# Loading q, k and v of the second group ahead of the weights, and issuing later q and k loads behind the transposing DMAs

## The chip, the cores and the metric

One core of a Trainium2 chip. The metric is the device time of one execution in microseconds (us); a time is the median of repeated runs, and the kernel before is timed on the same chip beside each variant.

The engines are called as in the profile: PE does matmuls, DVE vector work, ACT functions such as GELU (the profile of before has 21 table loads of 1.28 us, which come where the program changes the function), GpSimd (POOL) and SyncE (SP) issue DMAs here.

## The reference, cut to what matters

A gated linear attention runs over 4 batches of 768 positions, 8 heads of 48. Its output x (3072 tokens of 384) goes through a gated GELU layer of width 1536.

```python
for t in range(S):                                  # S = 768; the kernel takes 3 "groups" of 256 positions per batch, 12 in all
    S_re, S_im = a_t * (S_re, S_im) + k_t v_t^T     # complex decay a, after normalising |a|
    y_t = q_t . S_re
x   = y as 3072 x 384
out = x + sigmoid(x @ w_res) * ((gelu(x @ w_gate) * (x @ w_val)) @ w_out)
```

## The kernel before

q, k, a_re and a_im arrive as float32 rows of 48 numbers, so in pieces of 192 bytes. Group g needs a(g), q(g), k(g) and v(g). The a, q and k loads and the stores of `ot` are issued from SyncE's queue; v, the weights and the second stores to the output (`x`, added to what `ot` left) from GpSimd's. `held(..., after)` makes an issue wait until an earlier load has landed; `issue_after` only orders the building of the program.

```python
def ramp():                      # groups 0 to 4: decay, cumulative sums, first attention
    ...                          # -- cut --
    load_q(1, T["ld", "w", 1])   # q, k of group 1: behind the second pair of weight loads
    a0 = attention_first(g0, 0, 0)
    ...                          # -- cut: csl(g1), ex(g1), csl(g2), ex(g2), squares of groups 3, 4 --
    with tc.issue_after(T["row"].ins):
        load_q(2, T["ld", "w", 2])   # q, k of group 2: behind the third pair
    load_w_out()                     # w_out: behind q of group 2
    ...
    with tc.issue_after(T["ld", "k", 2].ins):
        load_a(5)

def mk(nm, src):                 # later groups: padded products, transposed by DMA
    ...
    if g >= TURN:                # TURN = 5
        nc.sync.dma_start_transpose(out=tt, in_=pads[nm, g % 2])   # QT, KT

for g in range(3):
    load_a(g)
load_q(0)
for g in gs(2):                  # groups 3 and 4
    load_a(g)
load_v(0, T["ld", "ai", 2])
for i in range(4):
    load_w_in(i, T["ld", "k", 0])     # a pair (w_gate, w_val) per i, behind k of group 0
load_v(1, T["ld", "w", 0])
load_w_res()
load_v(2, T["ld", "w", 1])
ramp()
for u in range(NU + 1):
    if u > 0:
        phase_x(u)               # output matmuls of unit u-1, decay sums of unit u+1
    ...
    phase_y(u)                   # gate and value matmuls of unit u, attention of unit u+1
    for g in gs(u + 2 if u == 0 else u + 3) + (gs(3) if u == 0 else []):
        load_q(g)                # two phases ahead
        after_landing(T["k", g], call(load_v, g))
```

There are 3 buffers for q and k. Units 1 to 5 hold two groups each. padQ and padK are the padded products of a group, QT and KT what the transposing DMAs make of them. I call the phase y of unit 0 "Y0", and the two in which transposes met other loads "Y2" and "Y3".

Of the kernel before, what the change touches and what calls it, by code (L numbers as in the profile page):

```python
# [28 lines left out]
def kernel(  # L29
# [13 lines left out]
    nc = tc.nc  # L43
# [55 lines left out]
    pads = {}  # L99
# [28 lines left out]
    T = {}  # L128
# [12 lines left out]
    def rows(a, g, c):  # L141
        b, s = ORD[g]
        t0 = (s * C + c) * 128
        return a[b, :, t0:t0 + 128, :].rearrange("h t d -> t h d")
# [4 lines left out]
    def held(i, after):  # L149

        if after is not None:
            tc.add_manual_dep(i.ins, after.ins.name, behind, reason="load order")
        return i

    def load_a(g, after=None):
        for nm, src, pool in (("ar", a_re, ldr), ("ai", a_im, lda)):
            t = pool.tile([128, C, H, D], FP, tag=nm, name=nm)
            for c in range(C):
                T["ld", nm, g] = held(nc.sync.dma_start(out=t[:, c], in_=rows(src, g, c)), after)  # L159
            T[nm, g] = t  # L160
        T["a"] = g + 1

    def load_q(g, after=None):
        for nm, src in (("q", q), ("k", k)):
            t = ldq.tile([128, C, H, D], FP, tag=nm, name=nm)
            for c in range(C):
                T["ld", nm, g] = held(nc.sync.dma_start(out=t[:, c], in_=rows(src, g, c)), after)
            T[nm, g] = t

    def load_v(g, after=None):  # L170
        t = ldv.tile([128, C, H, D], BF, tag="v", name="v")
        for c in range(C):
            held(nc.gpsimd.dma_start(out=t[:, c], in_=rows(v, g, c)), after)  # L173
        T["v", g] = t

    def load_w_in(i, after=None):

        FQ = FF // 4
        for w, src in ((wg, moe_w_gate), (wv, moe_w_val)):
            T["ld", "w", i] = held(nc.gpsimd.dma_start(  # L180
                out=w[:, :, i * FQ:(i + 1) * FQ],
                in_=src[:, i * FQ:(i + 1) * FQ].rearrange("(i p) m -> p i m", p=128)), after)
# [17 lines left out]
    def flat(t):  # L200
        return t.rearrange("p c h d -> p (c h d)")
# [31 lines left out]
    def p1_steps(g):  # L233

        def s0():
            lm = T["lm", g]
            act(out=lm, in_=lm, func=AF.Ln)
            nc.vector.tensor_scalar(out=lm, in0=lm, scalar1=0.5, scalar2=LNMAX, op0=OP.mult, op1=OP.min)  # L238

        def s1():  # L240
            ar = flat(T["ar", g])
            T["s", g] = pE.tile([128, W], FP, tag="E" if g == 1 else "Ei", name="ra") if g in (1, 2) else ar
            act(out=T["s", g], in_=ar, func=AF.Ln)

        def s2():
            T["th", g] = flat(T["ai", g])
            act(out=T["s", g], in_=T["s", g], func=AF.Exp, scale=-1.0)
            nc.vector.tensor_tensor(out=T["th", g], in0=T["s", g], in1=T["th", g], op=OP.mult)
        return [s0, s1, s2]
# [5 lines left out]
    def cs_l(g, c):  # L255
        if c == 0:
            if g == 0:
                t = hb.tile([128, 4, DM], FP, tag="sg", name="E0")
                T["E", g] = t[:, 0:2].rearrange("p a m -> p (a m)")
                T["Ei", g] = t[:, 2:4].rearrange("p a m -> p (a m)")  # L260
            else:
                T["E", g] = pE.tile([128, W], FP, tag="E", name="E")
                T["Ei", g] = pE.tile([128, W], FP, tag="Ei", name="Ei")
        sl = slice(c * DM, (c + 1) * DM)
        cs = psM.tile([128, DM], FP, tag="mm", padded_shape=[128, 512], name="csl")
        nc.tensor.matmul(out=cs, lhsT=lmat[c], rhs=T["lm", g][:, sl], start=True, stop=True)  # L266

        def ex():
            act(out=T["E", g][:, sl], in_=cs, func=AF.Exp)
            act(out=T["Ei", g][:, sl], in_=cs, func=AF.Exp, scale=-1.0)  # L270
        return ex
# [63 lines left out]
    def decay2(g):  # L335
        if g in NEXT.values():
            nc.gpsimd.dma_start(out=T["md", g][1:2, :], in_=T["Ei", g][0:1, 0:DM])
            turn("m2", g, T["md", g], 2)
        if g in NEXT:
            md = dr.tile([2, DM], FP, tag="d2", name="d2")  # L340
            T["row"] = (nc.sync if ORD[g][1] == 0 else nc.gpsimd).dma_start(out=md[0:1, :], in_=T["E", g][127:128, DM:W])
            T["md", NEXT[g]] = md
# [14 lines left out]
    def products(g):  # L357
        def x0():
            qE = flat(T["q", g]).bitcast(BF)[:, 0:W]
            nc.vector.tensor_tensor(out=qE, in0=flat(T["q", g]), in1=T["E", g], op=OP.mult)  # L360
            T["qE", g] = qE

        def x1():
            kE = flat(T["k", g]).bitcast(BF)[:, 0:W]
            nc.vector.tensor_tensor(out=kE, in0=flat(T["k", g]), in1=T["Ei", g], op=OP.mult)
            T["kE", g] = kE

        def mk(nm, src):
            def x():
                t = pads[nm, g % 2][:, :, 0:DD].rearrange("p x (u d) -> p x u d", u=2)  # L370
                sb = T[src, g].rearrange("p (x u d) -> p x u d", u=1, d=D).to_broadcast([128, C * H, 2, D])
                nc.vector.tensor_tensor(out=t, in0=T["CS", g], in1=sb, op=OP.mult)
                T[nm, g] = t
                if g >= TURN:
                    tt = trp.tile([128, C * H, 128], BF, tag=nm + "T", name=nm + "T")
                    nc.sync.dma_start_transpose(out=tt, in_=pads[nm, g % 2])
                    T[nm + "T", g] = tt
            return x
        return [x0, mk("Q", "qE"), x1, mk("K", "kE")]
# [247 lines left out]
    def gs(u):  # L627
        return UNITS[u] if 0 <= u < NU else []
# [7 lines left out]
    def call(f, *a):  # L636
        return lambda: f(*a)
# [56 lines left out]
    def ramp():  # L694

        g0, g1, g2 = gs(0) + gs(1)
        pend = {}

        def csl(g):
            pend[g] = [cs_l(g, c) for c in range(C)]  # L700

        def ex(g):
            for f in pend[g]:
                f()
            decay2(g)

        def cst(g):
            for c in range(C):
                cs_t(g, c)
        g3, g4 = gs(2)  # L710
        p = {g: p1_steps(g) for g in range(5)}
        q = {g: squares(g) for g in range(5)}
        pr = products(g0)

        def run(*fs):
            for f in fs:
                f()
        table("natural_log_exp_and_others")()
        run(*q[g0], p[g0][0], p[g0][1])
        csl(g0)  # L720
        run(p[g1][1], p[g0][2], q[g1][1], p[g1][2])
        ex(g0)
        run(p[g2][1], q[g2][1], p[g2][2])
        table("trig_and_small")()
        pr[0]()
        pr[2]()
        for g in (g0, g1, g2):
            if g > g0:
                T["f", g] = flat(T["ar", g])
            p1_arctan(g)  # L730
            cst(g)
            if g == g0:
                run(q[g1][0], q[g1][2], q[g2][0], q[g2][2])
        p2_sin(g0)
        pr[1]()
        pr[3]()
        load_q(1, T["ld", "w", 1])
        a0 = attention_first(g0, 0, 0)
        table("natural_log_exp_and_others")()
        run(p[g1][0], p[g2][0])  # L740
        run(*a0[:2])
        csl(g1)
        csl(g2)
        run(*a0[2:4], *q[g3], p[g3][1], p[g3][2])
        ex(g1)
        run(*a0[4:7], *q[g4], p[g4][1])
        ex(g2)
        run(p[g4][2], p[g3][0], p[g4][0], call(decay0, g4), *a0[7:])
        with tc.issue_after(T["row"].ins):
            load_q(2, T["ld", "w", 2])  # L750
        load_w_out()
        table("trig_and_small")()
        p2_sin(g1)
        p2_sin(g2)
        with tc.issue_after(T["ld", "k", 2].ins):
            load_a(5)
        p1_arctan(g3)
        p1_arctan(g4)
# [21 lines left out]
    load_q(0)  # L780
    for g in gs(2):
        load_a(g)
    load_v(0, T["ld", "ai", 2])
    for i in range(4):
        load_w_in(i, T["ld", "k", 0])
    load_v(1, T["ld", "w", 0])
    load_w_res()
    load_v(2, T["ld", "w", 1])
    ramp()
    for u in range(NU + 1):  # L790
        if u > 0:
            phase_x(u)
        while T["a"] < min(NG, gs(u + 1)[-1] + 6 if gs(u + 1) else NG):
            load_a(T["a"])
        phase_y(u)
        for g in gs(u + 2 if u == 0 else u + 3) + (gs(3) if u == 0 else []):
            load_q(g)
            after_landing(T["k", g], call(load_v, g))


# [28 lines left out]
```

## Time and profile before

| | before |
|---|---|
| timed median | 318.36 us (3 runs) |
| span in the profile | 315.3 us |
| first gate matmul (timeline of PE) | 58.6 us |
| ACT idle for ar, DVE idle for ai, of group 4 | 9.2 us, 12.9 us |
| PE idle for KT in Y2 and Y3 | 3.8 us, 3.0 us |
| Y2, Y3 (GELU table load to next table load) | 26.0 us, 25.7 us |

Some rows of the page's part 2. Each digit is a fortieth of the span (7.9 us): busy tenths, or tenths of the full TensorE clock.

```profile
PE   0355436789698999799599999598999998999994
DVE  0789119899599997699477999477995866565452
PEclk9998766599989999999979999899999999999999
DMA  8999999999999996369997259984479505920541
GB/s 150 187 178 187 177 147 190 179 189 177 155 179 130 188 189 89 39 121 236 192 185 61 46 92 216 190 154 28 74 121 183 93 2 106 181 49 2 126 77 51
```

DMA is busy until about 118 us. DVE has a hole at slices 5 and 6 (31 to 47 us), and PE one at slice 20 and one at slice 26.

The waits of the whole run; columns are total us, times, longest.

```profile
ACT lm L212 <- DMA ar<-in_a_re_dram: 14.7, 3, 9.2
DVE sq L223 <- DMA ai<-in_a_im_dram: 14.1, 3, 12.9
PE at L437 <- DMA KT<-padK: 6.8, 2, 3.8
```

The first two are the hole in the ramp, the third the holes in Y2 and Y3. Here is SyncE's queue as Y2 begins (start us, length us):

```profile
142.51 0.99 SPq L167 DMA_DIRECT2D q<-in_q_dram  x2
143.93 2.51 SPq L167 DMA_DIRECT2D k<-in_k_dram  x2
146.49 1.04 SPq L617 DMA_DIRECT2D out_dram<-ot  x1
147.57 3.18 SPq L376 DMA_TRANSPOSE QT<-padQ  x1
150.81 3.47 SPq L376 DMA_TRANSPOSE KT<-padK  x1
154.38 3.60 SPq L376 DMA_TRANSPOSE QT<-padQ  x1
158.08 2.65 SPq L376 DMA_TRANSPOSE KT<-padK  x1
```

padQ was ready at 142.5 us, yet QT is issued 5 us later, behind a q load, a k load and a store. The next lines are the windows view: stretch and its length, busy us and number of instructions of PE, PEld (weight loads), DVE, ACT and POOL, and behind them the granted clock (PEclk), DMA share (time of the packets over that of 16 engines; it can pass 1) and GB/s. First Y2, Y3 and the phase after them (Y4), then two stretches of Y2 around PE's wait, and two of Y3.

```profile
143.10:169.10 26.00, 21.84 (x154) 11.71 (x155) 19.23 (x35) 14.04 (x25) 6.20 (x9) 0.93 1.23 187
187.90:213.60 25.70, 21.94 (x149) 11.34 (x151) 18.65 (x35) 12.40 (x21) 6.98 (x9) 0.93 1.18 184
233.60:254.60 21.00, 20.84 (x155) 11.27 (x157) 15.53 (x29) 11.64 (x21) 1.71 (x2) 1.00 0.70 126
...
154.00:158.00 4.00, 0.17 (x2) 0.05 (x2) 0.80 (x5) 1.35 (x3) 1.32 (x2) 1.00 1.57 228
158.00:162.00 4.00, 3.78 (x22) 2.25 (x24) 2.31 (x5) 0.60 (x1) 0.00 (x0) 0.57 1.41 127
...
199.00:203.00 4.00, 0.98 (x7) 0.41 (x6) 1.55 (x6) 1.48 (x3) 1.35 (x2) 0.94 1.46 207
203.00:207.00 4.00, 3.78 (x24) 2.17 (x26) 2.23 (x5) 0.60 (x1) 0.00 (x0) 0.64 1.30 222
```

### The profile page before, as it was taken

The numbers are of one execution on the slowest core, as the hardware profiler recorded it, in microseconds if no ns is written. First come the engines' busy times: TensorE is split into PE (matmuls) and PEld (weight loads), VectorE is DVE, ScalarE is ACT, GpSimd is POOL, SyncE is SP. The second block draws the span as 40 slices with busy tenths as digits, with TensorE's granted clock in tenths as the row PEclk, the third lists the DMA queues.
The fourth block names the chain that finished last, engine by engine and source line by source line (L and its number), as shares of the span: only waits on it lengthen the run. The fifth ranks groups of instructions, "written<-read, shape, count | busy, mean of one in ns | idle before, by whom it ended". The sixth has DMA issues, their size and how long they took to land.

```text
span 315.3 us, 5310 instructions
## 1 busy us (share of the span) xinstructions
PE 258.6 (82%) x1912; PEld 156.2 (50%) x1928; DVE 229.0 (73%) x412; ACT 200.3 (64%) x333; POOL 89.9 (29%) x133
## 2 busy tenths in 40 slices
PE   0355436789698999799599999598999998999994
PEld 0133214578354666464256654265654565445682
DVE  0789119899599997699477999477995866565452
ACT  3867075979989578976548974359664474456150
POOL 4075300310337322462503555103711122110220
PEclk9998766599989999999979999899999999999999
DMA  8999999999999996369997259984479505920541
GB/s 150 187 178 187 177 147 190 179 189 177 155 179 130 188 189 89 39 121 236 192 185 61 46 92 216 190 154 28 74 121 183 93 2 106 181 49 2 126 77 51
DMA packets 167427, 41.92 MB, mean 133 GB/s; under 512 B 156516, under 2 KB 167400, under 8 KB 167400
## 3 DMA queue, kind: packets, MB, share of 16 engines
q1 hardware_dynamic: 132424, 30.95, 58.0%
q0 software_dynamic: 34976, 10.63, 32.0%
q8 instruction: 15, 0.25, 0.3%
q14 instruction: 12, 0.10, 0.1%
HBM read 31.33 MB, written 9.08 MB: 128 GB/s over the span
## 4 chain that ended last, share of the span: by engine, by line
PE 55%; ACT 14%; DMA 14%; SPq 6%; DVE 6%; issue 4%; POOL 0%; ACTq 0%; DVEq 0%
PE op L610 14%; PE vp L590 11%; PE gp L586 11%; DMA ai<-in_a_im_dram 6%; DMA KT<-padK 5%; SPq L159 4%; PE cst L299 4%; PE cst L301 3%; PE rp L602 2%; ACT L624 2%; PE at L437 2%; ACT lm L139 2%; DMA v<-in_v_dram 2%; PE dk L479 1%; DMA ar<-in_a_re_dram 1%
## 5 line engine op out<-in xcount | busy, mean ns | idle before, releaser
L139 ACT ACTIVATE h<-gp 128x512 bf16<-128x512 f32 (+1 forms) x84 | 44.7, 536 | 51.7 <-PE gp L586 51.4
L593 DVE SCALAR_TENSOR_TENSOR h<-h,vp 128x512 bf16<-128x512 bf16 (+1 forms) x84 | 50.5, 607 | 22.2 <-PE vp L590 18.3
L590 PE MATMUL vp<-xT,wv 128*128 128x512 bf16 (+1 forms) x250 | 63.4, 357 | 0.2
L586 PE MATMUL gp<-xT,wg 128*128 128x512 bf16 (+1 forms) x238 | 62.0, 354 | 1.7 <-DVE xT L577 0.5
L610 PE MATMUL op<-wo,h 128*128 128x384 bf16 x288 | 52.2, 332 | 2.5 <-ACT Ei L139 2.5
L610 PEld LDWEIGHTS <-h 128*128 128x128 bf16 x288 | 27.8, 99 | 21.6 <-issue 5.8
L619 POOL DMA_DIRECT2D out_dram<-x x22 | 20.4, 958 | 59.1 <-DMA out_dram<-ot 50.7
L590 PEld LDWEIGHTS <-wv 128*128 128x128 bf16 x252 | 24.7, 100 | 20.9 <-issue 1.7
L586 PEld LDWEIGHTS <-wg 128*128 128x128 bf16 x252 | 23.9, 100 | 18.5 <-issue 1.7
L322 POOL DMA_DIRECT2D m<-d x32 | 23.5, 771 | 19.4 <-DMA d<-ar 7.4
L624 ACT ACT_TABLE_LOAD x21 | 26.9, 1283 | 1.1 <-PEq L813 0.7
L266 PE MATMUL csl<-lm,lt0a 128*128 128x384 f32 x24 | 12.4, 603 | 17.9 <-DVE lm L238 10.5
L173 POOL DMA_DIRECT2D v<-in_v_dram x24 | 21.7, 909 | 14.6 <-DMA ai<-in_a_im_dram 11.9
L440 DVE TENSOR_TENSOR atm<-at,mask 128x512 bf16<-128x512 f32 x28 | 19.2, 684 | 9.0 <-PE at L437 9.0
L196 POOL COPY landed<-k 1x1 f32<-1x1 f32 x9 | 2.8, 316 | 68.8 <-DMA k<-in_k_dram 68.8
L613 DVE SCALAR_TENSOR_TENSOR ot<-sg,op 128x384 f32<-128x384 f32 x24 | 13.2, 550 | 10.6 <-PE op L610 9.2
L212 ACT ACTIVATE lm<-ar 128x768 f32<-128x768 f32 x12 | 10.1, 840 | 14.7 <-DMA ar<-in_a_re_dram 14.7
L299 PE MATMUL cst<-ai,lt0b 128*128 128x384 f32 x24 | 11.8, 578 | 7.7 <-ACT ai L139 6.0
L492 ACT CAST x<-y 128x384 bf16<-128x384 f32 x22 | 10.6, 480 | 10.9 <-PE y L489 10.9
L437 PE MATMUL at<-QT,KT 96*128 96x128 bf16 x112 | 11.4, 224 | 7.3 <-DMA KT<-padK 6.8
L139 ACT ACTIVATE ar<-ar 128x768 f32<-128x768 f32 x20 | 16.7, 856 | 0.0
L230 DVE TENSOR_TENSOR lm<-lm,sq 128x768 f32<-128x768 f32 x12 | 11.4, 951 | 7.2 <-ACT sq L226 6.9
(112 smaller groups left out, 514.0 us busy)
## 6 DMA issues: line engine op xcount, KB each, us to landing
ar<-in_a_re_dram SPq DMA_DIRECT2D x24, 192.0 KB, 4.9
ai<-in_a_im_dram SPq DMA_DIRECT2D x24, 192.0 KB, 4.8
q<-in_q_dram SPq DMA_DIRECT2D x24, 192.0 KB, 4.6
k<-in_k_dram SPq DMA_DIRECT2D x24, 192.0 KB, 4.7
out_dram<-ot SPq DMA_DIRECT2D x24, 192.0 KB, 2.4
out_dram<-x POOLq DMA_DIRECT2D x22, 192.0 KB, 3.9
v<-in_v_dram POOLq DMA_DIRECT2D x24, 96.0 KB, 5.2
wg<-in_moe_w_gate_dram POOLq DMA_DIRECT2D x4, 288.0 KB, 8.8
```

What stands on the lines that cost most here:

```text
L139: return tab(nc.scalar.activation(**kw))
L173: held(nc.gpsimd.dma_start(out=t[:, c], in_=rows(v, g, c)), after)
L299: nc.tensor.matmul(out=cs, lhsT=tmat[c], rhs=th[:, sl], start=True, stop=(s == 0))
L322: nc.gpsimd.dma_start(out=m[u * D:(u + 1) * D].rearrange("p r h -> p (r h)"), in_=md.rearrange("r (h d) -> d (r h)", h=H))
L437: nc.tensor.matmul(out=at[:, j], lhsT=T["KT", g][0:DD, x0 + j], rhs=T["QT", g][0:DD, x0 + j], start=True, stop=True)
L440: nc.vector.tensor_tensor(out=atm, in0=at, in1=mask4, op=OP.mult)
L586: nc.tensor.matmul(out=gp, lhsT=wg[:, fi, ffi * 128:(ffi + 1) * 128], rhs=xT[:, fi, :], start=(fi == 0), stop=(fi == KD - 1))
L590: nc.tensor.matmul(out=vp, lhsT=wv[:, fi, ffi * 128:(ffi + 1) * 128], rhs=xT[:, fi, :], start=(fi == 0), stop=(fi == KD - 1))
L593: T["gmul"] = nc.vector.scalar_tensor_tensor(out=h2[:, ffi, :], in0=h2[:, ffi, :], scalar=0.5, in1=vp, op0=OP.mult, op1=OP.mult)
L610: nc.tensor.matmul(out=ps, lhsT=h2[:, ffi, jj * 128:(jj + 1) * 128], rhs=wo[:, ffi, :], start=(ffi == 0), stop=(ffi == KF - 1))
L619: nc.gpsimd.dma_start(out=out[t0:t0 + 128, :], in_=T["x", token(u, jj)], accum_op=OP.add)
L624: tab(nc.scalar.preload_act_table_set(nm))
```

## The change

Its intent: (1) in the ramp, q, k and v of group 1 load ahead of the weights, and the weights start only when q of group 1 has landed, so that they no longer slow the a loads; (2) later q and k loads are issued one phase ahead in place of two, and behind the transposes of the same phase.

```diff
-                    nc.sync.dma_start_transpose(out=tt, in_=pads[nm, g % 2])
+                    T["turn"] = nc.sync.dma_start_transpose(out=tt, in_=pads[nm, g % 2])
 ... in ramp()
-        load_q(1, T["ld", "w", 1])
 ... at the head
+    load_q(1)
     load_v(0, T["ld", "ai", 2])
+    load_v(1, T["ld", "ai", 4])
     for i in range(4):
-        load_w_in(i, T["ld", "k", 0])
-    load_v(1, T["ld", "w", 0])
+        load_w_in(i, T["ld", "q", 1])
+    load_v(2, T["ld", "w", 1])
     load_w_res()
-    load_v(2, T["ld", "w", 1])
 ... in the loop over the units
-        for g in gs(u + 2 if u == 0 else u + 3) + (gs(3) if u == 0 else []):
-            load_q(g)
+        for g in gs(u + 2):
+            with tc.issue_after(T["turn"].ins) if "turn" in T else nullcontext():
+                load_q(g)
             after_landing(T["k", g], call(load_v, g))
```

## The prediction

> **What bounds the kernel now.** Profile span 315.3 us (timed median 318.36), in stages:
> (a) Ramp, 0 to 58.6 us (first gate matmul, timeline). DMA is saturated: about 190 GB/s with 192-byte rows (DMA view, 3 to 15 us), where a, q and k loads of the SyncE queue land in a median 4.6 us. At 20 to 46 us, with the weight loads of the GpSimd queue running, ai needs 12.5 and ar 14.5 us. [...] So group 4's ar and ai come late: ACT idles 9.2 us before its square (31.0 to 40.2), DVE 12.9 us (32.9 to 45.8). Both are in the chain of waits (13.5 us DMA ai).
> (b) 58.6 to 143 us is compute (busy per window: DVE 20.9 of 22.4, ACT 17.7 of 19, PE 25.1 of 26). DMA stays saturated to about 118 us.
> (c) The phases with transposing DMAs at 143 to 169 and 188 to 213.6 us take 26.0 and 25.6 us with PE busy 21.8 of each; PE idles 3.8 and 3.0 us for KT (waits). Loads of q and k sit ahead of the transposes in SyncE's in-order queue: padQ is ready at 142.5, QT issues at 147.6, KT at 150.8, landing 7.1 us later. The same phase at 233 to 254, with no loads ahead, takes 21.0, PE 20.8 busy.
>
> **The change.** Instruction order on PE, DVE and ACT is identical, byte count too; only SyncE and GpSimd orders move.
> 1. Group 4's a loads no longer compete with weights, only with v0. Estimate from 1.06 us per 192 KB load: its ai lands near 30 us, q1 near 32. Both stalls vanish. ACT then meets csl of groups 1 (PE, 31.7 to 34.5) and 2, so the gain is under 12.9: following the chain, 10.3 us; first gate matmul near 48.
> 2. Weights start at 32.5 instead of 20; first pair lands near 38, last near 46, before use. But q2 waits for the third pair and lands near 48, at its use. DMA work up to k of group 3 (lands 81.9, used 88.0) is unchanged, so it can't come 10 us earlier: estimate 78 to 81 against a use at 77.7. I give back 2.5 us there and at q2.
> 3. Transposes issue as pads are ready, q and k loads follow. QT and KT come about 5 us earlier, uncontended; both phases shrink to about 22: gain 7.5 us. Later loads have slack.
>
> Gain 10.3 - 2.5 + 7.5 = 15.3. Predicted **303.0 us**, range 298 to 309. Faster by over 2% 0.93, within 2% 0.06, slower 0.01.
>
> **What would show it.** (1) Waits of ACT lm and DVE sq for DMA fall from 9.2 and 12.9 us to under 2 each; first gate matmul at 46 to 50. (2) New short DVE waits on DMA for q or k, 48 to 55 and 75 to 80 us; no waits for weights. (3) PE's wait before at<-QT,KT under 1 us in both phases, phases 21.5 to 23 us; QT issues within 1 us of padQ.
>
> **What would make it wrong.** Weights alone slower than mixed with other loads, so that gate matmuls, q2, wo and groups 5 and 6 arrive late and most of the ramp gain moves into the next phases: 307 to 310. Transposes held by out stores or a loads still ahead in SyncE's queue: up to 7 us less gain. More DMA slack than thought: 300. A lower granted clock in denser PE stages.

What the trace of before shows of the loads and the weights (DMA view): in the 12 us from 3 to 15 SyncE's queue alone moved 2.30 MB (192 GB/s); in the 12 us from 22 to 34 it moved 0.53 MB and the queue with the weights 1.73 MB, 188 GB/s in all. The 1.06 us per 192 KB load can be read from SyncE's queue: 12 loads were issued in the 12.7 us from 5.56 to 18.25.

## More of the kernel before

PE idles from 154 to 158 us; and in the 4 us after that the granted clock is 0.57, and a matmul of 128x512 takes nearly twice as long (starts 0.43 us apart at 159.5 us, 0.22 at 161.7). Y4 has no loads ahead of its transposes and runs at 1.00 throughout.

## The result, and the profile after

The changed kernel takes 303.03 us (302.32 to 303.73, 4 runs) against 318.12 us; the ratio is 0.952 with a 95% interval of 0.946 to 0.958. A ratio is the mean time of one kernel's runs over that of the other's of the same rounds, so not quite the ratio of the medians. Executions over 1.5% slower than the fastest of the same kernel are left out of the means. Two later groups of runs gave 302.94 us (0.955) and 303.03 us (0.956).

The total hit the predicted 303.0. The parts did not. Since the order of instructions on PE, DVE and ACT is the same in both kernels, the same events can be compared; ACT's table loads mark the stages:

| event | before, us | after, us | ahead by |
|---|---|---|---|
| first gate matmul | 58.6 | 45.8 | 12.8 |
| GELU table load of Y0 | 63.4 | 58.7 | 4.7 |
| table load that ends Y0 | 81.2 | 77.9 | 3.3 |
| table load that starts Y2 | 143.1 | 140.0 | 3.1 |
| the one that ends Y2 | 169.1 | 160.5 | 8.6 |
| the one that starts Y3 | 187.9 | 179.3 | 8.6 |
| the one that ends Y3 | 213.6 | 200.4 | 13.2 |
| end of the span | 315.3 | 302.0 | 13.3 |

So the first gate matmul is 12.8 us ahead, but only 3.1 us of that is left when Y2 starts; and Y2 and Y3 together give 5.5 + 4.6 = 10.1 us. (The profiled execution of before, 317.1 us, was quicker than its median, and that of the changed kernel, 303.7 us, the slowest of its four, so the spans differ by 13.3 us where the medians differ by 15.1.)

These are single executions. In the two later profiles of the changed kernel the first gate matmul came at 47.1 and 47.9 us, Y0 ended at 76.6 and 78.1 us, and the wait for q of group 2, described next, was 5.8 and 5.5 us; Y2 and Y3 took 20.5 and 21.1 us in all three.

```profile
PE   0344853499798999799999999989999998999994
DVE  0789990789589999599897998887976767564452
PEclk9999865589979999999999999999999999999999
DMA  9999999999999991049999679998599835910631
GB/s 147 187 175 186 138 199 197 168 187 195 174 171 183 205 174 5 4 87 210 190 171 174 54 124 172 214 182 64 74 205 197 109 40 112 185 26 2 156 57 53
```

DVE's hole at slices 5 and 6 is gone, but there is one in slice 7 and PE's slices 7 and 8 are low: a new wait at about 46 to 55 us. PE's holes at Y2 and Y3 are gone. The line of the new wait, from the waits view of the whole run, and the one that is left of the old wait, from the waits of the first 60 us:

```profile
DVE q L360 <- DMA q<-in_q_dram: 8.3, 1, 8.3
...
DVE sq L223 <- DMA ai<-in_a_im_dram: 1.3, 2, 0.9
```

DVE waits 8.3 us for q of group 2. That load may not be issued before the third pair of weights has landed, and this pair now starts 13 us later. SyncE's queue in the ramp, and then at Y2:

```profile
26.31 2.16 SPq L167 DMA_DIRECT2D q<-in_q_dram  x2
28.51 2.03 SPq L167 DMA_DIRECT2D k<-in_k_dram  x2
30.64 6.03 SPq L341 DMA_DIRECT2D d<-E  x3
46.27 1.10 SPq L167 DMA_DIRECT2D q<-in_q_dram  x2
...
139.40 3.06 SPq L376 DMA_TRANSPOSE QT<-padQ  x1
142.56 0.52 SPq L617 DMA_DIRECT2D out_dram<-ot  x1
143.17 4.03 SPq L376 DMA_TRANSPOSE KT<-padK  x1
147.29 2.10 SPq L376 DMA_TRANSPOSE QT<-padQ  x1
149.49 3.80 SPq L376 DMA_TRANSPOSE KT<-padK  x1
153.34 1.83 SPq L167 DMA_DIRECT2D q<-in_q_dram  x2
```

Between 36.7 and 46.3 us SyncE's queue stands still, waiting for weights; q of group 2 then lands near 54.0 us, 7.3 us after its issue. At Y2, QT is issued as padQ ends (139.37 us) and the q loads follow. The windows of Y2, Y3 and Y4, and three stretches of Y0:

```profile
140.00:160.50 20.50, 20.44 (x156) 11.02 (x155) 18.93 (x35) 13.95 (x25) 3.09 (x4) 1.00 1.22 194
...
179.30:200.40 21.10, 20.69 (x154) 10.97 (x152) 18.40 (x34) 12.41 (x22) 3.92 (x6) 1.00 1.23 191
...
220.20:241.30 21.10, 21.10 (x159) 11.32 (x158) 15.48 (x29) 11.64 (x21) 3.72 (x5) 1.00 1.02 173
...
43.00:58.00 15.00, 5.71 (x43) 3.92 (x41) 5.83 (x8) 6.38 (x9) 6.44 (x9) 0.50 1.30 185
58.00:62.00 4.00, 2.92 (x26) 2.57 (x25) 3.69 (x6) 3.10 (x5) 0.19 (x1) 0.50 1.21 175
62.00:66.00 4.00, 4.00 (x55) 3.59 (x53) 2.71 (x8) 1.73 (x4) 0.00 (x0) 0.83 1.27 185
```

Y2 and Y3 now look like Y4: about 21 us, PE busy all along, clock 1.00. PE does the same matmuls there in 20.4 and 20.7 us that took 21.8 and 21.9 us of busy time before; that this difference is the slower clock is tested below.

### The profile page after: what moved, and what is told of

Same layout as the page of the kernel before. It is cut to its first block, busy times and chain, and to the rows that moved or that the text cites. A ratio compares the mean times of both kernels' runs of the same rounds, so it can differ in the third digit from the quotient of the medians.

```text
span 302.0 us, 5306 instructions
## 1 busy us (share of the span) xinstructions
PE 254.6 (84%) x1928; PEld 154.2 (51%) x1928; DVE 228.6 (76%) x412; ACT 199.9 (66%) x333; POOL 90.3 (30%) x133
## 4 chain that ended last, share of the span: by engine, by line
PE 66%; ACT 14%; DMA 8%; issue 4%; DVE 3%; POOL 2%; SPq 1%; ACTq 0%; DVEq 0%
PE op L610 15%; PE gp L586 15%; PE vp L590 14%; PE cst L299 4%; PE rp L602 3%; PE cst L301 3%; DMA wv<-in_moe_w_val_dram 3%; DMA ai<-in_a_im_dram 3%; DMA q<-in_q_dram 2%; ACT L624 2%; PE at L437 2%; PE dk L479 2%; ACT lm L139 2%; ACT CS L139 1%; SPq L159 1%
## 5 line engine op out<-in xcount | busy, mean ns | idle before, releaser
L586 PE MATMUL gp<-xT,wg 128*128 128x512 bf16 (+1 forms) x252 | 62.9, 354 | 0.7 <-DVE xT L577 0.4
L173 POOL DMA_DIRECT2D v<-in_v_dram x24 | 23.1, 970 | 30.3 <-DMA ai<-in_a_im_dram 24.3
L613 DVE SCALAR_TENSOR_TENSOR ot<-sg,op 128x384 f32<-128x384 f32 x24 | 13.2, 550 | 10.6 <-PE op L610 9.2
L360 DVE TENSOR_TENSOR q<-q,E 128x768 bf16<-128x768 f32 x12 | 11.4, 954 | 12.2 <-DMA q<-in_q_dram 8.3
L266 PE MATMUL csl<-lm,lt0a 128*128 128x384 f32 x24 | 11.6, 567 | 10.5 <-DVE lm L238 10.5
L299 PE MATMUL cst<-ai,lt0b 128*128 128x384 f32 x24 | 11.1, 547 | 7.7 <-ACT ai L139 6.0
L455 ACT COPY qk<-tp 96x512 bf16<-96x512 bf16 x16 | 9.3, 582 | 11.6 <-PE dk L479 8.7
```

Of the source, the lines that this page charges most:

```text
L173: held(nc.gpsimd.dma_start(out=t[:, c], in_=rows(v, g, c)), after)
L299: nc.tensor.matmul(out=cs, lhsT=tmat[c], rhs=th[:, sl], start=True, stop=(s == 0))
L586: nc.tensor.matmul(out=gp, lhsT=wg[:, fi, ffi * 128:(ffi + 1) * 128], rhs=xT[:, fi, :], start=(fi == 0), stop=(fi == KD - 1))
L613: nc.vector.scalar_tensor_tensor(out=ot, in0=T["sg", u][:, jj], scalar=1.0, in1=ps, op0=OP.add, op1=OP.mult)
```

## The experiments

The twelve runs answered four questions: do the two parts add up, what gave the ramp's gain back, what exactly helps the transposes, and does the low clock matter.

### The two parts apart

The head of the change alone:

```diff
 (before)
-        load_q(1, T["ld", "w", 1])
+    load_q(1)                      # and v(1), the weights behind q(1), as in the change
     # later loads: left as before
```

> The kernel before with only the first part of the change (q, k, v of group 1 ahead of the weights). Theory, from comparing the two traces: the gain of 12.8 us at the first gate matmul is almost all given back by an 8.3 us wait of DVE for q of group 2, whose load is held behind the third weight pair, so only about 3 us remain: 315 us, first gate matmul near 46, q wait 8 us, KT waits of PE 3 to 4 us as before in both transposing phases. Rival, the split of my prediction: the ramp keeps 7.8 us and the transposes bring the rest: 310 us.

Measured: 313.5 us, ratio 0.989 (0.984 to 0.994), so 3.5 us. The first gate matmul came at 47.3 us and DVE waited 6.1 us for q of group 2. PE waited 6.4 us for KT in two waits. 

The later loads alone:

```diff
 (before; T["turn"] is set as in the change)
-        for g in gs(u + 2 if u == 0 else u + 3) + (gs(3) if u == 0 else []):
-            load_q(g)
+        for g in gs(u + 2):
+            with tc.issue_after(T["turn"].ins) if "turn" in T else nullcontext():
+                load_q(g)
```

> The kernel before with only the second part (later q and k loads one phase ahead and behind the transposes). Theory from the traces: about 10 us (phases of 26.0 and 25.7 us become 20.5 and 21.1): 308 us; the ramp is as before (first gate matmul at 58.6, DVE waits 12.9 us for ai). Rival, the split of my prediction: 7.5 us, 310.5. If the two parts add up, the gains of this run and of the head alone sum to the 15 us of the whole change; if they interact, they don't.

Measured: 306.95 us, ratio 0.967 (0.962 to 0.973), so 10.4 us. First gate matmul at 58.5 us, DVE wait for ai 13.2 us, Y2 and Y3 20.5 and 21.1 us. The two gains sum to 13.9 us, and the whole change gives 14.0 to 15.3 by its three ratios. Within the noise the parts add up, about a quarter to three quarters. My split of the prediction, half to half, falls.

### What gave the ramp's gain back

First the gate of q(2):

```diff
 (changed)
-            load_q(2, T["ld", "w", 2])
+            load_q(2, T["ld", "w", 0])
```

> The changed kernel, with the loads of q and k of group 2 held behind the first pair of weight loads in place of the third. Theory: the gate is what makes q2 late; q2 then issues near 38 to 40 us in place of 46, lands near 45 to 47, and the 8.3 us wait of DVE shrinks to under 2: gain 4 to 8 us over the changed kernel, 295 to 299 us. Rival: DMA is full in this stretch, so an earlier q2 makes weights, wo and groups 3, 5 and 6 later, waits reappear there and the total stays within 2 us of 303.

Measured: 301.48 us, ratio 0.950 (0.945 to 0.955). q(2) was issued at 39.4 us, 7 us earlier, but took 11.1 us to land (DMA view, median of its two loads; 7.3 in the changed kernel), so DVE still waited 4.6 us, against 5.5 to 8.3 in the three profiles of the changed kernel. From 38 to 52 us the queue with the weights moved 1.95 MB and SyncE's 0.55 MB, 181 GB/s in all. My theory of the gate alone falls and the rival holds for the total: within 2 us of 303. The earlier issue was mostly spent on a slower transfer beside the weights.

Then the weights' gate:

```diff
 (changed)
-        load_w_in(i, T["ld", "q", 1])
+        load_w_in(i, T["ld", "k", 0])
```

> The changed kernel with one gate undone: the weights start behind k of group 0 again, at 20 us, as before; q of group 1 stays early in SyncE's queue and the second part of the change stays. Theory: the late a loads of group 4 come from sharing DMA with the weights, so the DVE wait for ai returns at about 10 to 13 us and the first gate matmul falls back to 56 to 60 us; total 305 to 308 (as the second part of the change alone, 307). Rival: the place of q1 in SyncE's queue made the difference; then the first gate matmul stays near 46 and the total at 303.

Measured: 304.58 us, ratio 0.962 (0.955 to 0.969). (By the build, v of groups 1 and 2 also went behind the weights in GpSimd's queue.) The waits came back, from the waits view of 20 to 80 us:

```profile
ACT lm L212 <- DMA ar<-in_a_re_dram: 13.5, 2, 11.0
DVE sq L223 <- DMA ai<-in_a_im_dram: 10.9, 1, 10.9
```

The first gate matmul fell back to 56.9 us. So it is the weights, moving at the same time, that make a(4) late (SyncE's queue moved 0.53 MB in 12 us beside them and 2.30 MB in 12 us without them, in before), and not the place of q(1) in SyncE's queue. But the total is only 1.6 us worse than the changed kernel of the same group (303.03), less than I expected, and the intervals of the two ratios overlap (0.955 to 0.969, and 0.951 to 0.961): there is no wait for q(2) in this version. The gate that moves the first gate matmul by 9 to 11 us is worth little in the total; it moves the wait from a(4) to q(2). What the early q(1) and v are worth by themselves was not tested.

Then q(2) ahead of the weights:

```diff
 (changed)
     load_q(1)
+    load_q(2)
 ... in ramp()
-        with tc.issue_after(T["row"].ins):
-            load_q(2, T["ld", "w", 2])
```

> The changed kernel with q and k of group 2 issued right after those of group 1, so ahead of the weights in time (the weights still wait for q of group 1 only). The run with the gate at the first weight pair showed q2 in flight for 12 us, because weights and q2 share DMA; it gained only 1.5 us. Theory: what is missing is bytes, not the gate alone; with q2 and k2 loading before most weights, the DVE wait for q falls under 1 us, and the first weights still come by 46 us; the phase after the ramp starts some 8 us earlier, and I expect 296 to 299 us, with part of the gain lost to DMA-bound arrivals of groups 5, 6 and 3. Rival: the weights or wo come late in their place and the total stays at 301 to 303.

Measured: 301.17 us, ratio 0.950 (0.945 to 0.954), where the changed kernel of the same group has 302.94. The wait for q(2) was gone and the GELU table load came at 51.6 us (57.4 in the changed kernel of the same group), but Y0 ended at 75.3 us, only 1.3 us earlier (76.6). Again the rival was right on the total. PE now waited for v of group 2, and ACT for ar; the clock was 0.57 from 58 to 62 us. From the waits of PE at 43 to 75 us, and of the whole core at 28 to 95 us:

```profile
PE dk L479 <- DMA v<-in_v_dram: 1.8, 2, 1.2
...
POOL m L322 <- DMA d<-ar: 10.5, 1, 10.5
...
ACT lm L212 <- DMA ar<-in_a_re_dram: 2.3, 1, 2.3
```

The middle line matters: a row of 1.5 KB (the decay of group 4, d<-ar) was issued from GpSimd's queue at 48.7 us behind weights, v(2), w_res and a third of w_out, and landed only 13.7 us later, near 62.4. It reads a buffer that a load of ar waits for, and SyncE's queue stood until 62.5.

Last, all of these moved together:

```diff
 (the kernel with q(2) ahead of the weights)
     load_v(1, T["ld", "ai", 4])
+    load_v(2, T["ld", "ai", 4])
-    load_v(2, T["ld", "w", 1])
 ... in ramp(): load_w_out() moved behind load_a(5)
-                 T["ld", "q", 2])      # w_out behind q(2)
+                 T["ld", "ai", 5])     # w_out behind a(5)
```

> The kernel with q and k of group 2 ahead of the weights gained only 1.8 us over the change, though its wait for q2 was gone: in its trace PE waits 1.8 us for v of group 2, the clock drops once more, and the square of group 6 waits, because the slot of ar is freed by a small decay-row DMA that took 14 us to land behind wo on the GpSimd queue. This version also loads v of group 2 ahead of the weights and wo only behind the a loads of group 5. Theory: both waits go, 295 to 298 us. Rival: DMA is simply full up to k of group 3, each wait removed returns as another, and the total stays at 300 to 302.

Measured: 298.3 us (297.19 to 298.42, 6 runs), ratio to before 0.940 (0.935 to 0.946); the yardstick of the same group, the changed kernel, has 303.03 us and 0.956. It just misses the range of 295 to 298 us. The wait for v(2) is gone, that for q(2) is 0.8 us; a wait of ACT for ar of 2.6 us stays. The decay row still took 9.4 us to land, but SyncE's queue waited only 0.6 us for it, where it had waited 6.4 us. Y0 ends at 71.6 us, 6.5 us earlier than in the changed kernel of the group (78.1), and the next phase gives part of that back. This version beats both kernels.

> The changed kernel as the yardstick of this group of runs: 303 us, about 0.955 of the kernel before.

Together: in both kernels DMA is busy at 90% or more in nearly every slice of the first 113 us, and in the first three of these versions a wait stayed or came back at another load. Of the orders tried, only the one closest to the order of use (q(2), k(2), v(2), weights, a(5), w_out) gave a further 4.7 us; how much of that is v(2) and how much w_out was not separated.

### What helps the transposes

```diff
 (changed)
         for g in gs(u + 2):
-            with tc.issue_after(T["turn"].ins) if "turn" in T else nullcontext():
-                load_q(g)
+            load_q(g)
```

> The changed kernel without the ordering of the later q and k loads behind the transposes; they are still issued one phase ahead only. By the build, SyncE's queue then has the loads of the phase behind the transposes at 140 us anyway, and at the next transposing phase one half of a load between two transposes of its second group. Theory A: what counts is that no load stands right ahead of the first transposes, so one phase ahead does nearly all: 303 to 305 us, KT waits of PE under 1 us. Theory B: the explicit order is needed: KT waits return, 307 to 312.

Measured: 302.95 us, and 302.94 for the changed kernel beside it. Y2 and Y3 take 20.5 and 21.1 us and there is no wait for KT. The explicit order adds nothing; theory A holds.

> The changed kernel once more, as the yardstick of this group of runs: 303 us, about 0.952 of the kernel before.

```diff
 (changed)
-        for g in gs(u + 2):
+        for g in gs(u + 2 if u == 0 else u + 3) + (gs(3) if u == 0 else []):
```

> The changed kernel with the later q and k loads issued two phases ahead as before, but behind the most recent transposes emitted. By the build a pair of q and k loads stands right ahead of the first transposes of each phase again. Theory A (position in SyncE's in-order queue): KT waits of 3 to 4 us and the low granted clock after them return in both phases, about 10 us: 312 to 314. Theory B (the explicit order is what helps): 303 to 305.

Measured: 312.89 us, ratio 0.985 (0.980 to 0.991), as theory A has it. PE waited 5.2 us for KT in two waits, of 3.6 and 1.6 us. It was right on the total, not on every detail: Y2 took 27.0 us at a clock of 0.87, but Y3 only 22.8 us at 1.00, so the low clock did not return there. The explicit order behind the latest transposes is useless if a load of two phases ahead then stands in front of the next ones.

### Does the low clock matter

The kernel before, with PE's idle time in front of KT filled:

```diff
 (before)
                 at = psA.tile([128, 4, 128], FP, tag="at", name="at")
+                if g in (5, 7) and c == 0 and hg == 0:
+                    with tc.issue_after(T["rpm"].ins):          # the last matmul on w_res
+                        for r in range(14):                     # overwritten by the next ones
+                            nc.tensor.matmul(out=at (as 128 x 512), lhsT=wg[:, 0, 0:128],
+                                             rhs=wv[:, 0, 0:512], start=True, stop=True)
```

> The kernel before with 14 matmuls of no use (3.0 us at full clock) put on PE just ahead of the first score matmuls of groups 5 and 7, where PE stands idle 3.8 and 3.0 us for KT; they are overwritten, the result stays right. Theory: after such an idle stretch the granted clock is near 0.57 to 0.64 for some 4 us, which costs about 1.5 us more per phase; filling it keeps the clock at 1.00 and the phases shrink from 26.0 and 25.7 to about 24.5 and 24.2, total 315 us (3 us less) although PE does 6 us more work. Rival: the slow matmuls after the wait come from the DMA traffic or from semaphore waits; then the filling changes nothing or costs time, 318 to 321.

Measured: 315.22 us, ratio 0.993 (0.989 to 0.998), so about 2 us faster with 28 more matmuls. Y2 and Y3 of its profile, and the stretches around the filled place in Y3:

```profile
143.20:169.50 26.30, 23.42 (x169) 12.24 (x169) 19.21 (x35) 14.07 (x25) 5.16 (x7) 1.00 1.30 190
188.30:212.40 24.10, 23.53 (x162) 12.29 (x164) 18.64 (x35) 12.40 (x22) 6.07 (x9) 1.00 1.19 197
...
199.00:203.00 4.00, 3.95 (x20) 1.96 (x20) 2.29 (x8) 1.90 (x4) 1.35 (x2) 1.00 1.27 278
203.00:207.00 4.00, 4.00 (x46) 2.47 (x45) 2.56 (x5) 1.43 (x3) 0.00 (x0) 1.00 0.86 159
```

The last line answers to the one of before that had 0.64: the clock is 1.00. DMA is less busy in it (0.86 against 1.30), so it alone would not exclude DMA as the cause; but in the line above DMA moves 278 GB/s at a clock of 1.00, and over the whole of Y2 and Y3 it moves as much as before (190 and 197 GB/s against 187 and 184). Without the 3.0 us of filling, PE's busy time is 20.4 and 20.6 us, as in the changed kernel, where before had 21.8 and 21.9. Y3 went from 25.7 to 24.1 us, as the theory has it. Y2 took 26.3 us because in this execution KT came later, so that PE still waited 2.7 us after the filling; its clock stayed at 1.00 too, and from the arrival of KT to the end of the phase it took 9.5 us in place of 11.1 (Y3: 9.2 in place of 10.7). The rival, that DMA or semaphores made the matmuls slow, falls.

The same idea on the wait for q(2) in the changed kernel:

```diff
 (changed, before the first transposes of group 1 on PE)
+    for r in range(34):
+        T["dm"] = nc.tensor.matmul(out=dm (128 x 384), lhsT=wg[:, 0, 0:128], rhs=wg[:, 0, 0:384], ...)
     # and the products of groups 1 and 2 on v ordered behind them
```

> The changed kernel with 34 matmuls of no use (into a PSUM tile that nothing reads) on PE in the 7.4 us in which it waits for the products that wait for q2. The order of a few small matmuls after them changes slightly. Theory: the granted clock of 0.50 to 0.83 up to 66 us in the changed kernel comes from that idle stretch; filled, it is near 1.00 right after, and the next table change (77.9 us) comes 1 to 2 us earlier: total 301 to 302, 1 to 2 us under the changed kernel. Rival: DVE and DMA set the pace there, so the clock costs nothing: 303.

Measured: 301.84 us (300.50 to 303.17), the changed kernel beside it 303.03; the intervals of the two ratios overlap (0.946 to 0.957, and 0.951 to 0.961). It is inconclusive: the build put other small matmuls first, so PE then waited 2.7 us for another product and ran slowly again (clock 0.84 from 58 to 62 us, 0.73 from 62 to 66), and the wait for q(2) was 5.0 us (5.5 in the profile of the changed kernel beside it), not the 8.3 us that the filling was made for.

## Why the prediction was right or wrong

That the total was hit to 0.1 us was luck: two terms were mis-sized in opposite directions. The ramp kept 3.3 us in place of 7.8, the transposing phases gave 10.1 in place of 7.5. In the profiles this makes 13.4 us, not 15.3; the rest of the hit lies in the difference between these executions and the medians.

- **"Both stalls vanish ... first gate matmul near 48."** Right: 45.8 us, 12.8 us ahead where the prediction had 10.3 (47.1 and 47.9 in the later profiles). ACT's wait for ar of group 4 is gone; one of 2.9 us for group 3 is in both kernels (2.6 before). ACT waited only 0.8 us for the cumulative sums of group 1. That the weights caused the stalls was shown by starting them early again: waits of 11.0 and 10.9 us, first gate matmul at 56.9. The landing time of q(2), 11.1 us when issued earlier beside the weights and 7.3 in the changed kernel, agrees.
- **"q2 waits for the third pair and lands near 48, at its use ... I give back 2.5 us there and at q2."** This is the step that failed in size. The third pair landed at 46.3 us and q(2) near 54.0; DVE waited 8.3 us. Of 12.8 us, 3.3 were left at the end of Y0: 9.5 us given back, not 2.5 (7.0 and 7.7 by the two later profiles). Between the 38 and 46 that I gave for the first and last pair, the third would land near 43; it and the landing of q(2) after it were each about 3 us later, and I had set q(2)'s use at 48, when it was 45.8. I had named DMA being full as a limit, but at k of group 3; it bound earlier. No wait for q or k of group 3 appeared at 75 to 80 us.
- **"Gain 7.5 us" in the transposing phases.** The mechanism was right: QT is issued within 0.1 us of padQ in both phases, PE's wait for KT is gone. The size was 10.1 us, phases of 20.5 and 21.1 where I gave 21.5 to 23. The missing term is the clock: I counted PE's idle time and left out the slow matmuls after it (0.57 and 0.64 in the 4 us that follow). In before these followed waits of 3.8 and 3.0 us; filling the idle time kept the clock at 1.00. From how long a wait on the clock falls was not shown (see the last section). I had the clock row of the profile, and warned of the clock only in the wrong direction ("a lower granted clock in denser PE stages"); the denser stages had the higher one (Y2 with PE busy for 20.4 of 20.5 us at 1.00, before for 21.8 of 26.0 at 0.93).
- **What is not settled.** About 1.4 us more (1.4 and 2.4 in the later profiles) were lost in Y0 after q(2) had come, while the clock was at 0.50 to 0.83 up to 66 us; before, it was at 1.00 from 63.4. That the clock is the cause there is argued, not shown: the run made for it was inconclusive. And how the 9.5 us divide between the gate and the sharing of DMA was not separated further than the four orders of loading above.

## What to carry to other kernels

While DMA is full (here at 90% or more in nearly every slice of the first 113 us), moving one load forward can, as here, only move the wait to another; compare an event well behind the change (here the end of Y0), not the first one that comes earlier (here the first gate matmul), and order the loads by the time of their use. In before QT, whose padQ was ready at 142.5 us, was issued at 147.6, behind a q load, a k load and a store of its queue: keep loads for later phases out of the place right ahead of what the current phase waits for. Issuing them one phase later was enough (302.95 us without the explicit order, 302.94 with it). Here a wait of PE of 3 to 4 us cost about 1.4 us of busy time more than itself, since the matmuls after it ran at a lower clock (0.57 and 0.64; PE was busy for 21.8 and 21.9 us, and for 20.4 and 20.6 with the wait filled, without the filling); look at the clock row next to the hole.

## What was measured beside it, and is not explained

- After which waits of PE the clock fell. In before, waits of 3.8 us (Y2) and 3.0 us (Y3) were followed by a clock of 0.57 and 0.64 over the next 4 us, while waits of 2.7 us (Y2 with the wait filled) and 1.6 us (Y3 with loads two phases ahead) were followed by 1.00. In the run that filled the wait for q(2), PE was slow again after a wait of 2.7 us (clock 0.73 from 62 to 66 us). So the same length went both ways, and these runs give no length of wait from which the clock falls; none of them varied the length alone.
- Loads in pieces of 192 bytes on SyncE's queue landed in 4.6 us (median, 3 to 15 us of before) without the weight loads on GpSimd's, and beside them in 12.5 (ai) and 14.5 us (ar; 20 to 46 us of before).
- A small DMA behind large ones of its own queue: the 1.5 KB decay row took 13.7 us from issue to landing behind weights on GpSimd's queue (q(2) ahead of the weights), and held up a buffer; it took 7.3 us in the changed kernel and 9.4 in the fastest version. That the large ones ahead of it were the cause is likely, not shown.
